# Reordering the first batch of a fused attention and feed-forward kernel: loads, products and value copies

## The chip, the cores and the metric

The kernel runs on one core of a Trainium2 chip. The metric is the device time of one execution in microseconds. Five engines work side by side, each through its own instruction queue in order: TensorE (PE, matmuls and transposes into PSUM), VectorE (DVE), ScalarE (ACT), GpSimd (POOL) and SyncE (SP). GpSimd and SyncE also issue the transfers (DMAs) between device memory and the on-chip memory SBUF; the loads that turn float32 into bfloat16 are all issued by GpSimd.

## What is computed

Eight batches of windowed attention, eight heads of 64 channels, 576 tokens each, followed by a feed-forward layer over all 4608 tokens. Heads 0 to 3 ("plain") see the 32 tokens up to their own; heads 4 to 7 ("dilated") see every fourth token back, 32 of them.

```python
scores = scale * np.matmul(q, k.transpose(0, 1, 3, 2))
mask_plain = (rel >= 0) & (rel < window)                       # window 32
mask_dil = (rel >= 0) & (rel < window * dilation) & (rel % dilation == 0)   # dilation 4
...
attn = np.exp(scores); attn = attn / (np.sum(attn, axis=-1, keepdims=True) + 1e-09)
x = attn_out.transpose(0, 2, 1, 3).reshape(B * S, H * D)       # 4608 x 512
h = np.maximum(x @ w_in, 0.0)                                  # w_in 512 x 2048
return (h * h @ w_out).astype(np.float32)                      # w_out 2048 x 512
```

## The kernel before

The four head pairs are numbered e = 0 to 3; pairs 0 and 1 are plain, 2 and 3 dilated. The attention output of pair e is rows kt = e of a transposed activation `xT`, so a feed-forward matmul (line 939) multiplies one pair's rows (kt) with 128 columns of `w_in`; four of them, kt 0 to 3, complete a piece. Its results pass a relu on ScalarE (line 952) and a square on VectorE (line 955), and the second layer (line 986) multiplies them with `w_out`.

The first batch is cut into part 0 (tokens 0 to 255) and part 1 (the other 320). The feed-forward layer starts with tiles of 256 tokens. The function `ffn_groups` gives a tile's work as a list of groups. In the first tile a unit u is two pieces of 128 columns, and the first six groups are halves: group 0 does units 0 and 1 with kt 0 and 1 (the plain pairs), group 1 the same units with kt 2 and 3, groups 2 and 3 units 2 and 3 likewise, groups 4 and 5 units 4 and 5. Group 16 is the first group of the second tile, tokens 256 to 511, with kt 2 and 3, and so needs part 1 of the dilated pairs. The lists at lines 1139 and 1140 set the order of the groups: 0, 1, 2, 3, 16, 4, 5, 17 and so on. Relu and square of units 0 and 1 of the first tile are held back, until the codes `r` (relus) and `R` (squares).

All else in the first batch is ordered by hand, in the text PROGRAM (line 21): codes, and a bar after which the next feed-forward group runs. Everything ahead of the first bar comes before group 0. Each engine takes its share of the codes in this order. The codes:

- `L0:q001` and the like (line 166): loads of q and of k of batch 0; the first digit is the part, the rest are pairs, so `q101` is part 1 of the plain pairs. Two DMAs each.
- `L0:v0d`, `L0:v1d` (line 197): values of the dilated pairs, part 0 and 1, two DMAs each into a staging tile `vd`; `L0:v1s`, `L0:v1t` (line 189): values of plain pair 0 and 1, part 1, straight into the block tile `vbd`, two DMAs each. `L0:i...` loads a quarter of w_in, with `a` or `b` half of its rows (line 1057), and `L0:o...` a quarter of w_out. `L0:i0` is the whole first quarter.
- `T`, `C`: transposes of q and k of one pair and part on TensorE, and the copies from PSUM; `C..a` puts the first copy on ScalarE, `C..v` on VectorE (lines 752 to 779). `B` and `S`: bias and scores; `E`: exponential on ScalarE, with a mask product on VectorE in part 1 (line 824); `P` and `D`: products with the values, and denominators; `L`, `X`, `M`: logarithm and exponential for the reciprocal on ScalarE, and the final product on VectorE into `xT` (line 884). A code's two digits are pair and part; L, X and M of pairs 0 and 2 in part 0 stand for both pairs of their kind.
- `G20` and the like: spreading of a dilated pair's staged values into `vbd` for part 1 (two copies of 64 x 256, line 229); the last digit is the part of the values, and part 1's products need both. `h`: casts of the plain values, part 0, into `vbd`. `N`, `z`, `y`: zeroing. `u` and `m`: masks of part 1 and others. `f`: a load of the mask for later batches, issued by SP. `w`, `W`, `s`: filler matmuls on zeros.

A tile in PSUM or SBUF comes from a pool with few buffers: the pool `pf` has four, which the scores of part 0, products, and the feed-forward units use in turn, and a new tile waits until the former user of its buffer is through. `pa` has two.

GpSimd's queue in the first 40 us holds the loads of batch 0, the weights, the first loads of batch 1, and the memsets `z` and `y`. SP's queue holds the plain values of part 0 (line 1025), two small value loads, the mask of `f`, and later stores and transposing DMAs (`L2:x` and so on).

Of the kernel before, what the change touches and what calls it, by code (L numbers as in the profile page):

```python
# [18 lines left out]


PROGRAM = (
    "L0:q001 L0:q023 L0:q123 L0:v0d L0:i0 L0:q101 L0:v1d L0:i1a L0:i1b L0:v1s L0:i2a L0:v1t L0:i2b L0:i3 L0:o0 L0:o1 L0:o2 L0:o3 "
    "L1:q00123 z y L1:v0dp L1:q10123 s34x151 T00 C00a T10 C10a B00 B10 w1 S00 E00 B20 W1 S10 E10 N u B30 W1 w1 T20q "
    "w1 T20k C20v T30 C30v h W1 w1 S20 E20 w1 S30 E30 T21 C21v T31 C31a G20 G30 P00 P10 D00 D10 L00 X00 P20 P30 "
    "D20 D30 L20 X20 M00 j S21 S31 w1+31 M20 E21 E31 G21 G31a | T01q T11q | T01k C01v r T11k C11a R P21 P31 D21 D31 S01 S11 L21 "
    "X21 M21 L31 X31 M31 E01 E11 | L2:q00123 L2:q10123 L1:v1dpr | | P01 D01 L01 X01 M01 P11 D11 L11 X11 M11 | | | "
    "| | | | | | | | | m n f | | | | | | 1q1 1q3 | 1q2f 1k2f | 1k1a 1v3 | 1a2 | 1v2 1k0a 1q0v | 1o2 | 1a0 1a1 | 1k3 "
    "1o0 1o1f | 1a3 1Q0 | 1K0 1o3 | 1Q1 1K1 | 1Q2 | 1b0 | | 1Q3 1K2 L2:vwp L3:q00123 L3:q10123 L2:vwdr | L2:x | | "
    "| | 1V2 | 1b2 1p0 | 1b1 1V3 1K3 | L3:x | 1p2 1p1f | 1b3 | 2t0 2t1 1p3f | | | L3:Vd0 L3:V1a L4:q00123 L4:q10123 "
    "L3:V1b | | | | | | | | | | L4:x | | | | | | | | | | | | | | | | | | L4:Vd L5:q10123 L5:q00123 L4:V01 | | | "  # L30
    "| | | | | | | | | | | | | L5:x | L5:Vd L6:q10123 L6:q00123 L5:V01"
# [31 lines left out]
def kernel(  # L63
# [9 lines left out]
    nc = tc.nc  # L73
# [28 lines left out]
    NF = DFF // P  # L102
# [57 lines left out]
    def staged(b: int, nm: str):  # L160


        t = rb[STAGE[b]][nm]
        return t[:, :].rearrange("p (a h x) -> p a h x", h=H, a=2)

    def load_qk(b: int, part, es):
        hs = slice(2 * es[0], 2 * es[-1] + 2)
        for nm, src in (("q", q), ("k", k)):
            t = staged(b, nm)
            t0, n = RES * MS[part], MN[part]  # L170
            nc.gpsimd.dma_start(  # L171
                t[0:n, part, hs, :], src[b, hs, t0 : t0 + RES * n, :].rearrange("h (p r) d -> p h (r d)", r=RES)
            )
# [50 lines left out]
    def spread_v(b: int, e: int, parts, copy=nc.vector.tensor_copy):  # L224

        p0, p1 = parts[0], parts[-1] + 1
        for hl in range(2):
            rows = slice(64 * hl, 64 * hl + 64)
            copy(
                vbd[b % 2][rows, e, RES * p0 : RES * p1, rows],  # L230
                vds[b][rows, e - NE // 2, p0:p1, :].rearrange("p m (r d) -> p (m r) d", d=D),
            )
# [200 lines left out]
    def step(b: int, code: str):  # L433

        what, e, home = code[0], int(code[1]), code[2:]
        part = int(what in "QKVbp")
        his = (0,) if "l" in home else (1,) if "h" in home else (0, 1)
        if what in "qk" and (b > XB or b == XB and e >= NE // 2):  # L440
            t = (qx if what == "q" else kx)[b % 2]
            halves(e, what, t[:, 2 * e : 2 * e + 2, :, :], 0, M, copier(what, e, home), his)
        elif what in "qQkK" and "h" in home:
            halves(e, what.lower(), *ready[b, e, what.lower()], his)
        elif what == "t":
            trans_both(e)
        elif what in "qQkK":
            trans(b, e, what.lower(), part, home)
        elif what in "vV":
            spread_v(b, e, [part] if b in PARTED else [0, 1])  # L450
        elif what in "ab":
            scores(b, e, part)
        elif "f" in home:
            pv(b, e, part, ps_f, "pf")
        else:
            pv(b, e, part)
# [265 lines left out]
    def turn(n: int, cols: int, at=None):  # L722


        if at:
            to = first["S", at[0], at[1]]
        else:
            to = first["W"] = first.get("W") or ps_o.tile([P, 512], f32, name="po")
        rhs = idle[:, :].unsqueeze(1).broadcast_to([P, cols // 256, 256]) if cols > 256 else idle[:, 0:cols]
        for _ in range(n):  # L730
            nc.tensor.matmul(
                to[:, 0:cols], idle[:, 0:P], rhs, start=not at, stop=not at, skip_group_check=True
            )
# [272 lines left out]
    def zero_halves(t):  # L1006
        nc.vector.memset(t[0:64, :, :, 64:128], 0.0)
        nc.vector.memset(t[64:128, :, :, 0:64], 0.0)
# [30 lines left out]
    def masks(part):  # L1039
        md = r4(mask_d[:, 256:704])  # L1040
        if part:
            put(r4(mask_p[:, 352:384]), near[:, :, 16:24])
            put(mask_p[:, 384:768].rearrange("p (i c) -> p i c", c=96), mk[:, 0:96].unsqueeze(1).broadcast_to([P, 4, 96]))
            put(r4(mask_p[:, 768:832]), near[:, :, 0:16])
            put(md[:, :, 0:32], mk[:, 224:256].unsqueeze(1).broadcast_to([P, RES, 32]))
            put(md[:, :, 32:112], mk[:, 160:240].unsqueeze(1).broadcast_to([P, RES, 80]))
            put(mask_d[:, 704:768], mk[:, 96:160])
            return
        put(mask_p[:, 0:288].rearrange("p (i c) -> p i c", c=96), mk[:, 0:96].unsqueeze(1).broadcast_to([P, 3, 96]))
        put(r4(mask_p[:, 288:352]), near[:, :, 0:16])  # L1050
        mf = mask_f[:, 0:320].rearrange("p (r c) -> p r c", r=2)
        put(mf[:, :, 0:80], mk[:, 176:256].unsqueeze(1).broadcast_to([P, 2, 80]))
        put(mf[:, :, 80:160], mk[:, 160:240].unsqueeze(1).broadcast_to([P, 2, 80]))
        put(mask_f[:, 320:384], mk[:, 96:160])
        put(r4(mask_d[:, 0:256]), mk[:, 160:224].unsqueeze(1).broadcast_to([P, RES, 64]))
# [20 lines left out]
    def run(code):  # L1076
        if code == "y":
            for nm in "qk":
                nc.gpsimd.memset(staged(1, nm)[64:80, 0, :, :], 0.0)
                nc.gpsimd.memset(staged(2, nm)[64:80, 0, 0 : H // 2, :], 0.0)  # L1080
        elif code == "z":
            nc.gpsimd.memset(vbd[1][0:64, :, :, 64:128], 0.0)
            nc.gpsimd.memset(vbd[1][64:128, :, :, 0:64], 0.0)
        elif code in "mu":
            masks(int(code == "u"))
        elif code == "R":
            while held:
                held.pop(0)[1]()
        elif code == "r":
            for relu, _ in held:  # L1090
                relu()
        elif code == "N":
            zero_halves(vbd[0][:, NE // 2 :, 0:8, :])
        elif code[0] == "G":
            spread_v(0, int(code[1]), [int(code[2])], nc.scalar.copy if code[3:] else nc.vector.tensor_copy)
        elif code == "h":
            for rows in sides:
                nc.vector.tensor_copy(vbd[0][rows, 0:2, 0:4, rows], plain[rows, :, :, :])
        elif code == "j":
            for rows in sides:  # L1100
                nc.vector.tensor_copy(vbd[0][rows, 2:4, 8, rows], tail[rows, :, :])
        elif code == "n":
            zero_halves(kbd)
        elif code == "f":
            nc.sync.dma_start(mask_n[:, :], near_dram.ap())
        elif code[0] == "s":
            turn(*(int(x) for x in code[1:].split("x")))
        elif code[0] in "wW":
            n, _, at = code[1:].partition("+")
            turn(int(n), 512 if code[0] == "w" else 256, [int(x) for x in at])  # L1110
        elif code[0] in "TCBSEPDXM" or code[0] == "L" and code[2:3] != ":":
            first_step(code)
        elif code[0] != "L":
            step(int(code[0]), code[1:])
        else:
            b, what, part, which = int(code[1]), code[3], code[4:5], code[5:]
            if what == "V":
                load_v_rows(b, code[4:] or "d01")
                return
            if what == "q":  # L1120
                load_qk(b, None if part == "w" else int(part), [int(e) for e in which])
            elif what == "x":
                cross_all(b)
            elif what == "v":
                load_v(b, [0, 1] if part == "w" else [int(part)], which)
            else:
                (load_w_in if what == "i" else load_w_out)(int(part), *[which][: len(which)])
# [6 lines left out]
    groups, steps = [], []  # L1134
# [1 line left out]
        groups += ffn_groups(tk0, nt)  # L1136

    head = groups[:G]
    groups[:NF] = [head[y] for y in (0, 1, 2, 3, 16, 4, 5, 17, 18, 19, 20, 21, 6, 7, 22, 23)]
    groups[NF:G] = [head[y] for y in (8, 9, 12, 13, 10, 11, 14, 15)] + head[24:32]  # L1140
    for x, code in enumerate(("R00", "R01", "R10", "R11")):
        steps.append((46, 0, XB, code))
# [5 lines left out]
    for b in range(NATURAL, B):  # L1148
# [12 lines left out]
        if b < PAIRED:  # L1161
            start = 61 if early else t - 8
            second = t + (7 if early else 5)
            x = 3 if early else 0
# [89 lines left out]
```

## Time and profile before

| | us |
|---|---|
| median of 3 runs | 299.52 (299.28 to 300.28) |
| the profiled execution | 298.59 |
| its span in the profile | 296.8 |
| TensorE busy | 289.8 (98%) |
| VectorE / ScalarE / GpSimd busy | 166.8 / 192.0 / 129.2 |
| first feed-forward matmul | 14.55 after the span's start |
| start of the fifth feed-forward group (units 4 and 5) | 23.09 |

All times inside an execution are counted from the start of its span. A timeline line gives start, length, engine, line of the kernel, operation, what is written from what, and in brackets the engine's idle time before it with what released it. The chain of waits goes back from the last instruction, at each step to what released it. A load's landing is the time at which its last byte was there.

### The profile page before, as it was taken

How to read it: one execution, taken by the hardware profiler on the slowest of the kernel's cores; microseconds unless marked ns; L12 is line 12 of the kernel's file. 1: busy time of each engine (PE TensorE's matmuls, PEld its weight loads, DVE VectorE, ACT ScalarE, POOL GpSimd, SP SyncE). 2: the span in 40 equal slices, each digit the busy share in tenths (PEclk: the TensorE clock that was granted, in tenths of full speed). 3: DMA queues.
4: the chain of work that ended last, by engine and by line, in shares of the span. 5: the costliest groups of instructions: out<-in, count | busy, mean ns of one | idle time of the engine just before them, and what ended most of it. 6: DMA issues, size and time to landing. Idle time of an engine off the chain costs nothing.

```text
span 296.8 us, 7869 instructions
## 1 busy us (share of the span) xinstructions
PE 289.8 (98%) x3156; PEld 169.7 (57%) x3183; DVE 166.8 (56%) x508; ACT 192.0 (65%) x397; POOL 129.2 (44%) x210
## 2 busy tenths in 40 slices
PE   8999999999999999999999999999999999999995
PEld 7689657868755554555455445545554455445543
DVE  2785566967869565686749474957445234005400
ACT  6897568757958665888667667766676567126511
POOL 8689882686695265855883687100000000000000
PEclk9999999999999999999999999999999999999999
DMA  8999999999989999979999599112101200121022
GB/s 126 202 188 213 204 152 229 182 163 186 180 101 172 195 130 178 155 128 173 167 195 148 66 171 170 11 38 73 38 0 33 77 35 0 38 71 35 0 74 71
DMA packets 82964, 35.37 MB, mean 119 GB/s; under 512 B 52608, under 2 KB 78176, under 8 KB 82928
## 3 DMA queue, kind: packets, MB, share of 16 engines
q0 software_dynamic: 49024, 18.40, 54.9%
q1 hardware_dynamic: 33760, 16.38, 27.8%
q8 instruction: 25, 0.41, 0.6%
q10 hardware_dynamic: 144, 0.10, 0.1%
q14 instruction: 11, 0.09, 0.1%
HBM read 37.31 MB, written 9.44 MB: 157 GB/s over the span
## 4 chain that ended last, share of the span: by engine, by line
PE 91%; DMA 4%; issue 1%; ACT 1%; POOL 1%; DVE 0%; ACTq 0%; POOLq 0%
PE pf L939 42%; PE pf L986 41%; DMA vd<-in_v_dram 2%; DMA kb<-in_k_dram 2%; PE po L661 2%; PE pf L661 1%; PE pa L661 1%; PE pd L661 1%; PE pa L277 1%; ACT h2T L952 0%; POOL qb L171 0%; PE po L414 0%; PE pa L357 0%; PE pa L351 0%; PE pd L416 0%
## 5 line engine op out<-in xcount | busy, mean ns | idle before, releaser
L986 PE MATMUL pf<-w_out_sb,h2T 128*128 128x512 bf16 (+2 forms) x572 | 127.5, 373 | 1.3 <-issue 0.5
L939 PE MATMUL pf<-xT,w_in 128*128 128x512 bf16 (+1 forms) x697 | 128.0, 340 | 0.6 <-DVE xT L884 0.2
L939 PEld LDWEIGHTS <-w_in 128*128 128x128 bf16 x704 | 77.9, 113 | 46.6 <-issue 0.5
L952 ACT ACTIVATE h2T<-pf 128x512 bf16<-128x512 f32 x144 | 83.7, 600 | 29.2 <-PE pf L939 28.8
L955 DVE TENSOR_TENSOR h2T<-h2T 128x512 bf16<-128x512 bf16 x144 | 60.2, 424 | 60.0 <-ACT h2T L952 57.6
L986 PEld LDWEIGHTS <-h2T 128*128 128x128 bf16 x592 | 55.5, 98 | 61.6
L992 ACT COPY osb<-pf 128x512 f32<-128x512 f32 (+1 forms) x34 | 19.5, 574 | 49.7 <-PE pf L986 49.6
L478 POOL DMA_DIRECT2D vbd<-in_v_dram x80 | 42.9, 546 | 20.0 <-DMA qb<-in_q_dram 7.1
L171 POOL DMA_DIRECT2D qb<-in_q_dram x18 | 13.0, 722 | 12.7 <-DMA xx<-qb 11.0
L684 ACT ACTIVATE rec<-rec 128x576 f32<-128x576 f32 x24 | 16.4, 682 | 0.7
L698 ACT ACTIVATE pt<-pa 128x384 bf16<-128x384 f32 (+1 forms) x28 | 12.7, 498 | 6.1 <-DVE xT L689 3.6
L192 POOL DMA_DIRECT2D vbd<-in_v_dram x16 | 11.0, 693 | 8.1 <-DMA kb<-in_k_dram 3.8
L687 DVE TENSOR_TENSOR xT<-po,rec 128x512 bf16<-128x512 f32 x14 | 9.7, 691 | 7.6 <-ACT rec L684 7.3
L465 POOL DMA_DIRECT2D vd<-in_v_dram x20 | 12.1, 614 | 3.8 <-PE pf L661 1.1
L171 POOL DMA_DIRECT2D kb<-in_k_dram x18 | 12.8, 710 | 1.5 <-issue 1.0
L470 POOL DMA_DIRECT2D vbd<-in_v_dram x20 | 11.9, 611 | 3.2 <-PE pf L939 1.1
L700 DVE TENSOR_TENSOR pt<-pt,mask_n 128x448 bf16<-128x448 bf16 (+1 forms) x20 | 7.1, 373 | 9.5 <-ACT pt L698 9.4
L700 DVE TENSOR_TENSOR pt<-pt,mask_f 128x384 bf16<-128x384 bf16 x24 | 8.4, 355 | 6.0 <-ACT pt L698 5.9
L687 DVE TENSOR_TENSOR xT<-pf,rec 128x512 bf16<-128x512 f32 x10 | 6.9, 692 | 8.7 <-ACT rec L684 8.7
L492 DVE COPY qT<-xx 64x576 bf16<-64x576 bf16 (+1 forms) x30 | 10.5, 349 | 0.6
L661 PEld LDWEIGHTS <-vbd 64*64 64x64 bf16 x288 | 7.6, 107 | 4.2 <-issue 3.8
L698 ACT ACTIVATE pt<-pf 128x448 bf16<-128x448 f32 (+1 forms) x18 | 8.5, 521 | 0.5 <-PE pf L661 0.3
(156 smaller groups left out, 317.0 us busy)
## 6 DMA issues: line engine op xcount, KB each, us to landing
qb<-in_q_dram POOLq DMA_DIRECT2D x7, 320.0 KB, 6.7
kb<-in_k_dram POOLq DMA_DIRECT2D x7, 320.0 KB, 8.1
vd<-in_v_dram POOLq DMA_DIRECT2D x32, 64.0 KB, 6.1
w_out_sb<-in_moe_w_out_dram POOLq DMA_DIRECT2D x4, 512.0 KB, 10.6
out_dram<-osb SPq DMA_DIRECT2D x16, 128.0 KB, 4.6
qb<-in_q_dram POOLq DMA_DIRECT2D x7, 256.0 KB, 8.5
kb<-in_k_dram POOLq DMA_DIRECT2D x7, 256.0 KB, 9.1
out_dram<-osb SPq DMA_DIRECT2D x9, 160.0 KB, 3.9
```

The lines of the kernel that those rows point to most:

```text
L171: nc.gpsimd.dma_start(t[0:n, part, hs, :], src[b, hs, t0 : t0 + RES * n, :].rearrange("h (p r) d -> p h (r d)", r=RES))
L478: nc.gpsimd.dma_start(v_rows[b % 2][p0 + 16 * r : p0 + 16 * r + 16, e, :, :], v[b, 2 * e + hl, :, :].rearrange("(i m r) d -> r m i d", r=R ...
L661: nc.tensor.matmul(out, lhs, rhs, start=begin, stop=True, skip_group_check=True)
L684: nc.scalar.activation(rec[:, :], rec[:, :], ACT.Exp, scale=-1.0)
L687: nc.vector.tensor_tensor(out=tok[:, :, 16:M], in0=byr(o[:, :]), in1=byr(rec[:, 0:512]), op=ALU.mult)
L698: nc.scalar.activation(pt, sp[b, e][g][:, 0:n], ACT.Exp, scale=SCALE)
L700: nc.vector.tensor_tensor(out=pt, in0=pt, in1=mask, op=ALU.mult)
L939: nc.tensor.matmul(to, w_in_sb[piece][:, kt, c0 : c0 + 509 : 4], rhs, start=(kt == kts[0] and x == 0), stop=(kt == kts[-1] and x == per - ...
L952: nc.scalar.activation(hv, acc[u][:, :].rearrange("p (x n) -> p x n", x=per), ACT.Relu)
L955: nc.vector.tensor_tensor(out=hv, in0=hv, in1=hv, op=ALU.mult)
L986: nc.tensor.matmul(cur[m][:, c0:c1], h2[:, f, P * m : P * m + P], w_out_sb[:, f, c0:c1], start=(f == 0), stop=(f == NF - 1),)
L992: (nc.vector.tensor_copy if last and part == 1 or tk0 == 3 * NT // 2 else nc.scalar.copy)(osb[:, c0:c1], cur[m][:, c0:c1])
```

## The change

- The first quarter of w_in is loaded in two halves (`i0a`, `i0b`), the staged dilated values of part 1 (`v1d`) come ahead of plain q and k of part 1 (`q101`).
- Three of the four spreads of dilated values move to GpSimd: `G20p` and `G30p` between the loads `i1b` and `v1s`, `G21p` between `v1s` and `i2a`. They were on VectorE (six copies). The fourth, `G31a`, stays on ScalarE.
- `h` comes ahead of B30; the plain products of part 0 (`P00 P10 D00 D10 L00`) come ahead of the dilated scores S20, S30 and of the transposes of part 1 of the dilated pairs (`T21`, `T31`); three fillers go; C31 is on VectorE.
- After group 1 come the relus, the dilated products of part 1, the squares, and only then the transposes of plain q and k of part 1, which stood before and after group 1. The plain scores of part 1 (`S01`, `S11`) stand after group 2, no longer before it.
- Group 16 comes ahead of group 3.
- `f` goes from among the first feed-forward groups to behind `L2:x`. SP ran it at 4.85 us, since nothing held it there.

```diff
-    "L0:q001 L0:q023 L0:q123 L0:v0d L0:i0 L0:q101 L0:v1d L0:i1a L0:i1b L0:v1s L0:i2a L0:v1t L0:i2b L0:i3 L0:o0 L0:o1 L0:o2 L0:o3 "
-    "L1:q00123 z y L1:v0dp L1:q10123 s34x151 T00 C00a T10 C10a B00 B10 w1 S00 E00 B20 W1 S10 E10 N u B30 W1 w1 T20q "
-    "w1 T20k C20v T30 C30v h W1 w1 S20 E20 w1 S30 E30 T21 C21v T31 C31a G20 G30 P00 P10 D00 D10 L00 X00 P20 P30 "
-    "D20 D30 L20 X20 M00 j S21 S31 w1+31 M20 E21 E31 G21 G31a | T01q T11q | T01k C01v r T11k C11a R P21 P31 D21 D31 S01 S11 L21 "
-    "X21 M21 L31 X31 M31 E01 E11 | L2:q00123 L2:q10123 L1:v1dpr | | P01 D01 L01 X01 M01 P11 D11 L11 X11 M11 | | | "
-    "| | | | | | | | | m n f | ...
+    "L0:q001 L0:q023 L0:q123 L0:v0d L0:i0a L0:i0b L0:v1d L0:q101 L0:i1a L0:i1b G20p G30p L0:v1s G21p L0:i2a L0:v1t L0:i2b L0:i3 "
+    "L0:o0 L0:o1 L0:o2 L0:o3 L1:q00123 z y L1:v0dp L1:q10123 s34x151 T00 C00a T10 C10a B00 B10 w1 S00 E00 B20 W1 S10 E10 N u h "
+    "B30 W1 w1 T20q w1 T20k C20v T30 C30v P00 P10 D00 D10 L00 S20 E20 S30 E30 X00 T21 C21v T31 C31v P20 P30 D20 D30 L20 X20 M00 j "
+    "S21 S31 w1+31 M20 E21 E31 G31a | | r P21 P31 D21 D31 R T01q T11q T01k C01v L21 X21 T11k C11a M21 L31 X31 M31 | "
+    "S01 S11 E01 E11 L2:q00123 L2:q10123 L1:v1dpr | | P01 D01 L01 X01 M01 P11 D11 L11 X11 M11 | | | "
+    "| | | | | | | | | m n | ...
-    "... | L2:x | | "
+    "... | L2:x f | | "
...
-            spread_v(0, int(code[1]), [int(code[2])], nc.scalar.copy if code[3:] else nc.vector.tensor_copy)
+            spread_v(0, int(code[1]), [int(code[2])], {"a": nc.scalar.copy, "p": nc.gpsimd.tensor_copy}.get(code[3:], nc.vector.tensor_copy))
...
-    groups[:NF] = [head[y] for y in (0, 1, 2, 3, 16, 4, 5, 17, 18, 19, 20, 21, 6, 7, 22, 23)]
+    groups[:NF] = [head[y] for y in (0, 1, 2, 16, 3, 4, 5, 17, 18, 19, 20, 21, 6, 7, 22, 23)]
```

## The prediction

> **What bounds the kernel now.** First the page's busy table and clock row: is one engine full, and is its clock whole?
>
> ```profile
> PE 289.8 (98%) x3156; PEld 169.7 (57%) x3183; DVE 166.8 (56%) x508; ACT 192.0 (65%) x397; POOL 129.2 (44%) x210
> PEclk9999999999999999999999999999999999999999
> ```
>
> TensorE is busy 98% of the span at full clock, so whatever is gained or lost must be TensorE's idle or filler time. Asked in stretches, TensorE is busy 268.4 of the 273.7 us after 23.1 us. The order of the instructions after that point is not changed. I therefore ask one thing: when does the fifth feed-forward group of the first batch (its units 4 and 5) start? Before, that is 23.09 us, after which TensorE runs nearly solid. A later or earlier start is passed on to the end one to one.
>
> Second, the chain of waits up to 25 us (start, length, what):
>
> ```profile
> 3.20 5.79 DMA kb<-in_k_dram
> 9.27 7.06 DMA vd<-in_v_dram
> 16.36 0.41 ACT vbd L229
> 16.79 0.40 ACT vbd L229
> 17.21 0.25 ACT h2T L952
> 17.71 0.59 ACT h2T L952
> 18.30 0.33 ACT xx L775
> 18.65 0.50 DVE xx L776
> 19.19 0.42 PE pa L813 x11
> 19.61 2.75 PE pf L939 x24
> ```
>
> The chain is a transfer, not arithmetic: the second part of the dilated values (the load v1d) lands at 16.33, two ScalarE copies spread it, two held relus queue behind them, then a copy of plain k, then the plain scores at 19.19. Only from 19.6 does TensorE stay full.
>
> Third, TensorE's own timeline, to see what it does meanwhile:
>
> ```profile
> 14.55 1.03 PE L939 MATMUL pf<-xT,w_in 128*128 128x256 bf16 x8 [0.16 <-DVE xT L884]
> 15.52 0.48 PE L761 MATMUL pa<-mk,qb 80*64 80x80 bf16 x16
> 17.33 0.45 PE L851 MATMUL po<-pt,vbd 128*128 128x32 bf16 x9
> 19.19 0.42 PE L813 MATMUL pa<-xx 64*64 64x32 bf16 x12 [0.35 <-DVE xx L776]
> ```
>
> Transposes of plain q and k (15.52 and 16.92) fill the time until the spread values are there; the products of part 1 of the dilated heads start at 17.33.
>
> Fourth, GpSimd's timeline, since the change puts copies into its queue:
>
> ```profile
> 11.37 1.42 POOL L1060 DMA_DIRECT2D w_in<-in_moe_w_in_dram  x2 [0.78 <-DMA kb<-in_k_dram]
> 12.77 0.72 POOL L192 DMA_DIRECT2D vbd<-in_v_dram  x1
> 14.55 0.67 POOL L192 DMA_DIRECT2D vbd<-in_v_dram  x1 [1.05 <-DMA w_in<-in_moe_w_in_dram]
> 15.42 0.74 POOL L1060 DMA_DIRECT2D w_in<-in_moe_w_in_dram  x1 [0.20 <-issue]
> 16.28 1.36 POOL L192 DMA_DIRECT2D vbd<-in_v_dram  x2
> ```
>
> Each issue takes 0.6 to 0.8 us, and the ninth load on waits for the landing of the one eight earlier (the load at 14.55 waited for the whole first quarter of w_in, landed 14.2). So this queue runs at the pace of the DMA.
>
> **The change, part by part** (times on the profile's clock).
>
> *Loads.* With w_in's first quarter in two loads and v1d ahead of plain q and k (q101), the first eight issues stay; the two halves go at 6.27 and 7.05, v1d at about 8.0 and 9.27 (its waits for loads 3 and 4 remain), q101 at 9.9 and 11.37 (waits for load 6), w_in's second quarter at 12.05 and 12.75. The last ends at 13.45. One more load is issued (0.75 us), where the queue waited anyway. By landed bytes (about 190 KB per us between 11.6 and 19.5), the first half lands near 12.9, the second at 14.2 as before, v1d 320 KB sooner, at 14.6 and 15.0, and q101 near 16.6 instead of 16.0. Moving the near mask's load (112 KB, issued by SP at 4.85, landed 10.95) behind batch 2's transposes takes it out of the first loads' way: between 0 and 112 KB at 195 GB/s, or 0.6 us; I take 0.4. Its first reader is at 103.9, against some 60 for the new place: nothing lost. So GpSimd is free at 13.45 - 0.4 = 13.05.
>
> *Plain products first.* The plain value casts (h, 0.86) move to 8.47, when the memsets are through and their last load has landed (8.2), ending 9.33 just before the transposes that VectorE waits for anyway: no cost. P00 P10 D00 D10 (0.8) follow the transposes' end at 9.6 and take the place of two 512-column and one 256-column filler. The first Ln is at 10.45, behind it E20 and E30 (0.35 apart) to 11.75, X00 to 12.4. C31 goes from ScalarE (0.69) to VectorE: 12.12 to 12.8. So M00 is at 12.8 to 13.5, against 13.81 to 14.50: one microsecond sooner, and M20 ends at 14.65 instead of 15.65. The first feed-forward group runs from 13.75 (its half of w_in is there), the second from 14.7 to 15.7 (before: 15.93 to 16.95).
>
> *Copies on GpSimd.* This decides. The part 1 products need all three spreads, G21p last. In the queue: four copies, two v1s loads (0.72 + 0.67), two copies. The trace has no GpSimd copy. Rows near it:
>
> ```profile
> L1080 POOL MEMSET qb<- 16x1024 bf16 x1 | 0.9, 945 | 0.0
> L1079 POOL MEMSET qb<- 16x2048 bf16 x1 | 1.8, 1797 | 0.0
> ```
>
> The difference is 0.83 ns per element and the rest 0.09 us, so writing 256 elements costs 0.31 us; reading and writing in turn would be 0.52. ScalarE takes 0.40 for this very copy, VectorE 0.22 to 0.33. Ends 0.22 and 0.52; I take 0.40, the same shape on the other engine without a doubled rate, which lies midway between the memset bounds. VectorE works on two SBUF operands meanwhile (the mask products, two of 0.40): a mutual delay of 0 to 0.8, taken as 0.2, since only part of them falls on the copies. Sum: 13.05 + 1.6 + 1.39 + 0.8 + 0.2 + 0.05 hand-over = 17.1. TensorE, through with the second group at 15.7, waits 1.4 us, and part 1 starts 0.2 sooner than before instead of 1.6. The two VectorE spreads (1.01 and 0.65) are saved off the path. ScalarE's G31a now ends about 15.6 and the relus 16.7: no longer the limit.
>
> For the price of the copy, the Trainium skill, GPSIMD Engine Reference, sections 3.1 and 4.1, calls one-input work roughly line-rate and its best loop 1.8 cycles per element; at its 1.2 GHz an estimate of 0.38 us, by which the sum would end 0.1 us sooner. No run so far shows it.
>
> *From part 1 to the fifth group.* Before: 23.09 - 17.33 = 5.76 us. Added: both pairs of transposes, 0.82, which earlier filled the wait, now stand behind part 1. Gone: the 0.35 wait for plain k ahead of 19.19, since a group stands between. New: the group on part 1 (units 0 and 1 of the next 256 tokens) is moved ahead of one group and needs the PSUM buffer that M31 frees. ScalarE does L21, X21, C11, L31, X31 after part 1 (five of about 0.45, C11 waiting for its transposes), then M31 comes 3.97 after part 1 starts, and TensorE would be there at 3.5: 0.45 lost. Sum 5.76 + 0.82 - 0.35 + 0.45 = 6.68, rounded to 6.65.
>
> The fifth group then starts at 17.1 + 6.65 = 23.75, 0.66 later than before. Behind G21p, w_in's third quarter is issued at 17.05 instead of 15.42 and v1t at 17.8 and 18.5 instead of 16.28. With the landing time before (5.6 and 5.1), they land at 22.65 and 23.6, with the 3.4 of an early load at 21.9; v1t is wanted at 23.3. I count nothing, with 0.3 as the upper end. GpSimd's later memsets move by some 1 us, but at 36.15 it waits for w_out again.
>
> The profiled execution took 298.59 (span 296.8), the median run 299.52, 0.93 more. The sum gives 299.25 against the former; against the median **300.2**.
>
> **Rivals.** *One, slower: GpSimd as the bound.* Copies of 0.52, the full 0.8 of collisions and no gain from the mask: 13.45 + 3.12 + 1.39 + 0.8 + 0.05 = 18.8, so the fifth group at 25.45, +2.4, 301.9; v1t late adds 0.3 to 0.8. For it: six copies stand in front of loads wanted soon. Against: the memsets run at 0.83 ns per element. It decides (beyond 0.3%) from 17.35, that is from 0.44 us per copy. Beside it stands the Trainium skill, SBUF — State Buffer, section "Who interferes with whom": VectorE work with two SBUF inputs and GpSimd's reads exclude each other for a whole instruction. GpSimd only writes and issues before, so no row shows that.
>
> *Two, faster: the copies are short.* At 0.22 each and 0.6 from the mask: 12.85 + 1.32 + 1.39 + 0.05 = 15.6, so part 1 starts at 15.7 right behind group two, the fifth group at 22.35, -0.75, 298.8. Break-even is a start at 16.45, a copy of 0.29 at my other values. For it: VectorE's rows. Against: even a pure write has 0.31.
>
> *Three: the idle stretch costs clock.* The granted clock is 1.00 in every stretch of before, thanks to fillers in the waits; 1.4 us is now empty. If the next 3 us ran at half rate: +1.5 more, 301.7. Against: the stretch from 18 to 20 us holds only 1.65 us of work, and its clock is 1.00.
>
> **How the numbers follow.** A tell-apart of about 0.3% (0.9 us) is what such a measurement allows. The forecast (part 1 at 16.5 to 17.9) has 0.55: 0.33 within 0.9 us, 0.22 beyond, slower. Rival one 0.19, slower. Rival two 0.22: its full price is short of 0.9 us, but loads landing sooner than I count would pass it: 0.12 faster, 0.10 same. Rival three 0.04, slower. Faster 0.12, same 0.43, slower 0.45. The range runs from rival two to rival one, 298.8 to 301.9; the forecast's own is 299.6 to 301.0.
>
> **What would show it.** First group near 13.75 and second ending near 15.7; six GpSimd copies near 0.4 us; an empty stretch on TensorE from 15.7 to about 17.1, released by GpSimd; M31 releasing the group after S11; the fifth group at 23.75. Copies under 0.3 or over 0.5 us, a wait of the fifth group or of P11 on a load, or a later stage that is not solid would make it wrong.

## The result and the profile after

| | before | after |
|---|---|---|
| median | 299.05 us (298.39 to 301.33, 22 runs) | 300.41 us (299.37 to 303.3, 22 runs) |
| ratio, with its 95% interval | | 1.0048 [1.0033, 1.0063] |
| start of the fifth feed-forward group (profiles) | 23.09 | 23.50, and 24.76 in a second profile |
| second half of w_in's third quarter issued, landed | 17.63, 22.9 | 19.23, 26.5 |

The change costs 1.36 us. The first profile of the changed kernel is of the slowest of its 22 runs (303.30 us, span 301.5); a second one, of a run at 300.11 us, stands below under "again". First the same two lines of the page as before, busy times and granted clock by fortieths of the span:

```profile
PE 292.6 (97%) x3180; PEld 170.1 (56%) x3180; DVE 166.5 (55%) x503; ACT 191.9 (64%) x396; POOL 132.7 (44%) x217
PEclk9997999999999999999999999999999999999999
```

The clock row has one digit below 9, in the fourth slice (22.6 to 30 us). Before it had none. GpSimd is busy 3.5 us longer. The chain of waits up to 27 us (start, length, what):

```profile
11.69 1.41 POOL w_in L1060 x2
...
13.15 0.40 POOL vbd L229
...
14.89 1.32 POOL vbd L192 x2
...
16.71 0.48 POOL vbd L229
17.20 0.68 POOL w_in L1060
17.88 1.35 POOL vbd L192 x2
19.23 7.29 DMA w_in<-in_moe_w_in_dram
26.51 0.05 issue
26.56 0.62 PE pf L939 x2
```

Read it upwards from the last line. TensorE's sixth group waited for a load of w_in; that load was issued at 19.23 because GpSimd's queue had been working through copies and other issues without a pause since 11.7. Before, the chain went through the staged values and ScalarE, and no load of w_in stood in it. These two lines of before are the ones to compare with, GpSimd's issue of the second half of that quarter (the first of the two) and TensorE's fifth group with all that follows it:

```profile
17.63 1.53 POOL L1060 DMA_DIRECT2D w_in<-in_moe_w_in_dram  x2
23.09 9.78 PE L939 MATMUL pf<-xT,w_in 128*128 128x256 bf16 x88
```

TensorE's timeline after the change shows the wait itself (start, length, operation, and in brackets the idle time before it and its releaser):

```profile
13.63 0.22 PE L813 MATMUL pf<-xx,kbd 64*64 64x64 bf16 x2 [0.90 <-issue]
14.31 1.91 PE L939 MATMUL pf<-xT,w_in 128*128 128x256 bf16 x16
17.25 0.42 PE L851 MATMUL po<-pt,vbd 128*128 128x80 bf16 x8 [1.02 <-POOL vbd L229]
23.50 1.04 PE L939 MATMUL pf<-xT,w_in 128*128 128x256 bf16 x8
26.56 10.58 PE L939 MATMUL pf<-xT,w_in 128*128 128x256 bf16 x80 [2.01 <-DMA w_in<-in_moe_w_in_dram]
```

Part 1 of the dilated heads starts at 17.25 behind GpSimd's last copy, and the fifth group at 23.50, only 0.41 later than before. Then, where there had been 9.78 us of solid work in 88 matmuls, eight run, TensorE stands for 2.01 us, and the other 80 take 10.58 us instead of 8.92 (the length they have in runs below at full clock). GpSimd's timeline:

```profile
13.15 1.74 POOL L229 COPY vbd<-vd 64x256 bf16<-64x256 bf16 x4
14.84 1.38 POOL L192 DMA_DIRECT2D vbd<-in_v_dram  x2
16.26 0.94 POOL L229 COPY vbd<-vd 64x256 bf16<-64x256 bf16 x2
17.14 0.74 POOL L1060 DMA_DIRECT2D w_in<-in_moe_w_in_dram  x1
17.88 1.38 POOL L192 DMA_DIRECT2D vbd<-in_v_dram  x2
19.23 1.53 POOL L1060 DMA_DIRECT2D w_in<-in_moe_w_in_dram  x2
```

The copies take 0.40 us each with 0.04 between them. w_in's third quarter goes out in two halves, at 17.14 and 19.23; before it was 15.42 and 17.63. The second half also took longer from issue to landing, 7.3 us instead of 5.3, and between 18 and 24 us the DMA carried 117 GB/s, where before it carried 185. Why the landing took longer is open. It is not the late issue alone: in the table below, three kernels that issue this half at 17.57 to 17.93 wait 6.2 to 6.9 us for it, and one that issues it at 18.62 waits 5.4.

### The profile page after: what moved, and what is told of

It is laid out like the page before. It is cut to its first block, busy times and chain, and to the rows that moved or that the text cites. A ratio compares the mean times of both kernels' runs of the same rounds, so it can differ in the third digit from the quotient of the medians.

```text
span 301.5 us, 7891 instructions
## 1 busy us (share of the span) xinstructions
PE 292.6 (97%) x3180; PEld 170.1 (56%) x3180; DVE 166.5 (55%) x503; ACT 191.9 (64%) x396; POOL 132.7 (44%) x217
## 4 chain that ended last, share of the span: by engine, by line
PE 83%; DMA 10%; POOL 5%; issue 1%; ACT 0%; POOLq 0%; ACTq 0%
PE pf L986 39%; PE pf L939 37%; DMA kb<-in_k_dram 6%; DMA w_in<-in_moe_w_in_dram 2%; DMA vbd<-in_v_dram 2%; PE po L661 2%; POOL vbd L192 1%; PE pf L661 1%; PE pa L661 1%; POOL qb L171 1%; POOL vbd L229 1%; PE pd L661 1%; POOL w_in L1060 1%; PE pa L277 1%; POOL kb L171 0%
## 5 line engine op out<-in xcount | busy, mean ns | idle before, releaser
L939 PE MATMUL pf<-xT,w_in 128*128 128x512 bf16 (+1 forms) x704 | 130.4, 344 | 2.2 <-DMA w_in<-in_moe_w_in_dram 2.0
L986 PE MATMUL pf<-w_out_sb,h2T 128*128 128x512 bf16 (+2 forms) x592 | 129.3, 373 | 0.0
L478 POOL DMA_DIRECT2D vbd<-in_v_dram x80 | 43.3, 551 | 18.8 <-DMA qb<-in_q_dram 7.6
L698 ACT ACTIVATE pt<-pa 128x384 bf16<-128x384 f32 (+1 forms) x28 | 12.8, 500 | 6.1 <-DVE xT L689 3.6
## 6 DMA issues: line engine op xcount, KB each, us to landing
w_out_sb<-in_moe_w_out_dram POOLq DMA_DIRECT2D x4, 512.0 KB, 12.4
```

The costliest lines, as they stand in the source:

```text
L478: nc.gpsimd.dma_start(v_rows[b % 2][p0 + 16 * r : p0 + 16 * r + 16, e, :, :], v[b, 2 * e + hl, :, :].rearrange("(i m r) d -> r m i d", r=R ...
L698: nc.scalar.activation(pt, sp[b, e][g][:, 0:n], ACT.Exp, scale=SCALE)
L939: nc.tensor.matmul(to, w_in_sb[piece][:, kt, c0 : c0 + 509 : 4], rhs, start=(kt == kts[0] and x == 0), stop=(kt == kts[-1] and x == per - ...
L986: nc.tensor.matmul(cur[m][:, c0:c1], h2[:, f, P * m : P * m + P], w_out_sb[:, f, c0:c1], start=(f == 0), stop=(f == NF - 1),)
```

## Experiments

Theory: the cost is the place of the copies in GpSimd's queue. They push back the issue of w_in's third quarter, whose second half had about one microsecond in hand (landed 22.9; the sixth group, 1.04 us after the start of the fifth, would have wanted it at 24.1). Rivals: the work of the copies costs by itself, each its share; the later start of part 1; the new order on the other engines; the idle stretches and the clock. In the diffs a line of code letters is cut to the part that differs. All ratios are against runs of the kernel before on the same chip.

| kernel | second half of third quarter issued, landed | fifth group | TensorE's waits after that, us | profiled run minus start of fifth group | ratio |
|---|---|---|---|---|---|
| before | 17.63, 22.9 | 23.09 | none | 275.50 | 1 |
| two spreads on GpSimd | 17.34, 22.6 | 22.82 | none | 275.72 | 1.0007 |
| fewer fillers | 17.57, 24.5 | 24.59 | none | 275.60 | 1.0017 |
| new order, copies on VectorE | 17.71, 24.5 | 23.78 | 1.14 for w_out | 277.70 | 0.9995 |
| mask late | 17.81, not recorded | 23.27 | none | 275.56 | 0.9974 |
| load order alone | 17.93, 24.1 | 23.52 | none | 275.58 | 0.9997 |
| mask twice | 18.51, 24.4 | 24.00 | 0.55 for w_out | 276.54 | 1.0027 |
| order alone | 18.62, 24.0 | 25.04 | none | 275.43 | 1.0043 |
| transposes in the gap | 18.78, 25.1 | 23.74 | 0.30 for w_in | 276.25 | 1.0046 |
| again | 19.12, 25.3 | 24.76 | none | 275.35 | 1.0042 |
| after | 19.23, 26.5 | 23.50 | 2.01 for w_in | 279.80 | 1.0048 |
| copies alone | 19.30, 25.7 | 23.06 | 1.64 for w_in, 0.30 for w_out | 277.95 | 1.0058 |
| hold the queue | 19.36, 26.7 | 23.82 | 1.89 for w_in | 277.64 | 1.0067 |
| last spread on GpSimd | 19.75, 26.0 | 24.07 | 0.95 for w_in | 276.83 | 1.0054 |

Below the kernel before, the table is sorted by the issue of that half. No kernel that issues it by 17.93 has an interval above 1; all that issue it from 18.5 on have. (In "order alone" and "mask twice" TensorE did not wait for it; there an earlier landing was late, which held up TensorE and this queue alike.) The last but one column confirms the way of reading of the prediction: where TensorE waits for nothing later, the time is the start of the fifth group plus 275.35 to 275.72 us.

**The changed kernel again.** No edit.

> The changed kernel once more, for a second profile. Start theory (part 1 of the dilated heads starts at 17.2 with TensorE idle from 16.1, the transposes stand behind it; the fifth feed-forward group is 0.4 us late and nothing more): the stall of the sixth group on w_in, 2.0 us in the first profile, is a stray of that execution and is under 0.5 us here; about 300.0. Queue theory (the GpSimd copies push the issue of w_in's third quarter from 15.42 and 17.63 to 17.14 and 19.23, so its second half lands after the sixth group wants it, near 24.4): the stall is here again, 0.5 to 2 us; about 300.4, ratio 1.0045.

Measured: 300.11 us (299.79 to 300.74), ratio 1.0042 [1.0027, 1.0058]. TensorE's timeline of this run:

```profile
14.45 0.22 PE L813 MATMUL pf<-xx,kbd 64*64 64x64 bf16 x2 [1.86 <-issue]
15.13 3.40 PE L939 MATMUL pf<-xT,w_in 128*128 128x256 bf16 x16
24.76 9.78 PE L939 MATMUL pf<-xT,w_in 128*128 128x256 bf16 x88
```

The wait for w_in is gone, but only because the fifth group is late for other reasons: TensorE stands 1.86 us for nothing that the profile names, the clock then falls and the first sixteen feed-forward matmuls take 3.40 us instead of 1.91. The half landed at 25.3, the sixth group began at 25.8. So one execution loses the time at 13 us, another at 24.5, and both end late. Neither theory expected this: the start theory has the missing wait right, but not the time, and the queue theory the time, but not the missing wait. Whatever TensorE does, the sixth group can't start before 25.3 to 26.5.

**The copies on VectorE again.** The changed kernel with the three spreads off GpSimd:

```diff
-L0:i1b G20p G30p L0:v1s G21p L0:i2a
+L0:i1b L0:v1s L0:i2a
-M20 E21 E31 G31a |
+M20 G20 G30 E21 E31 G21 G31a |
```

> The changed kernel with the three spreads back on VectorE, behind M20 (G20, G30) and behind the masks of part 1 (G21); all else as changed. Part 1 still starts near 17.1, so the start theory and the order theory expect the time of the change, ratio 1.003 to 1.005. Queue theory: GpSimd's queue issues w_in's third quarter at its old times, the stall is gone: 0.5 to 2 us less than the change, ratio 0.999 to 1.001.

Measured: 298.73 us (298.07 to 301.48), ratio 0.9995 [0.9968, 1.0023]. Undoing the copies alone takes the whole cost away. TensorE and GpSimd:

```profile
16.60 0.72 PE L851 MATMUL po<-pt,vbd 128*128 128x32 bf16 x9
23.78 9.78 PE L939 MATMUL pf<-xT,w_in 128*128 128x256 bf16 x88
```

```profile
17.71 0.77 POOL L1060 DMA_DIRECT2D w_in<-in_moe_w_in_dram  x1
```

Part 1 starts 0.65 earlier than with the copies on GpSimd, and the third quarter is out in time. The profiled run is the slowest of this kernel, with a wait of 1.14 for w_out at 39 us.

**The copies on GpSimd alone.** The kernel before, its order kept, with the three spreads in the queue:

```diff
-L0:i1a L0:i1b L0:v1s L0:i2a
+L0:i1a L0:i1b G20p G30p L0:v1s G21p L0:i2a
-C31a G20 G30 P00
+C31a P00
-E31 G21 G31a |
+E31 G31a |
```

> The kernel before, with G20, G30 and G21 on GpSimd at the places that the change gives them, and nothing else of it. Queue theory: the second half of w_in's third quarter is issued at about 19.4 instead of 17.63 and lands near 25, wanted at 23.97: TensorE stalls 0.5 to 2 us on w_in, 299.6 to 301, ratio 1.002 to 1.007. Start theory: G21 ends about 17.2 and part 1 starts at 17.33 as before, no stall: ratio 0.999 to 1.001. Order theory (the new order itself costs, whoever copies): ratio 1.000.

Measured: 300.49 us (298.9 to 304.49), ratio 1.0058 [1.0038, 1.0078]. GpSimd, then TensorE:

```profile
16.35 0.93 POOL L229 COPY vbd<-vd 64x256 bf16<-64x256 bf16 x2 [0.79 <-DMA vd<-in_v_dram]
...
19.30 1.55 POOL L1060 DMA_DIRECT2D w_in<-in_moe_w_in_dram  x2
```

```profile
17.55 0.45 PE L851 MATMUL po<-pt,vbd 128*128 128x32 bf16 x9
...
25.73 8.92 PE L939 MATMUL pf<-xT,w_in 128*128 128x256 bf16 x80 [1.64 <-DMA w_in<-in_moe_w_in_dram]
```

The copies alone make the whole cost, with part 1 only 0.22 later than before (17.33) and the fifth group on time at 23.06. A late part 1 is therefore not the cause.

**Holding the queue without the copies.** The kernel before, copies on VectorE; GpSimd instead fills a scratch tile that nothing reads (`H`), four times ahead of v1s and three times behind it, 0.42 us each:

```diff
+        elif code == "H":
+            nc.gpsimd.memset(mask_f[:, :], 0.0)
-L0:i1a L0:i1b L0:v1s L0:i2a
+L0:i1a L0:i1b H H H H L0:v1s H H H L0:i2a
```

> The kernel before, all copies where they were; GpSimd's queue is held by memsets of a scratch tile instead (0.41 us each by the memset rows): four behind i1b, three behind v1s. Nothing reads them. Queue theory (time in GpSimd's queue ahead of w_in's third quarter is the whole cost): its halves are issued near 17.1 and 19.2 as with the copies, the second lands near 25.5, the sixth group stalls 1 to 2 us, ratio 1.004 to 1.007, as pool_copies_alone. Port theory (the copies themselves, by sharing SBUF with VectorE or by their data coming late, are the cost): ratio 0.999 to 1.001.

Measured: 301.28 us (300.5 to 302.89), ratio 1.0067 [1.0045, 1.009]. GpSimd, then TensorE:

```profile
12.75 1.87 POOL L1082 MEMSET mask_f<- 128x384 bf16 x4
...
19.36 1.53 POOL L1060 DMA_DIRECT2D w_in<-in_moe_w_in_dram  x2
```

```profile
26.76 8.93 PE L939 MATMUL pf<-xT,w_in 128*128 128x256 bf16 x80 [1.89 <-DMA w_in<-in_moe_w_in_dram]
```

Work that no one waits for costs as much as the copies, within the intervals. What counts is that the queue is occupied in front of the third quarter's load. The fifth group was at 23.82 in this profile, 0.73 later than before, so not all of the profiled time is the wait for w_in.

**Four copies against two.** If the work of the copies counted, four would cost more than two. If the queue counts, it is the other way about, since the four lie where the queue had to wait for a landing anyway, and the two must themselves wait for the staged values. Both are the kernel before with one part of the move:

```diff
-L0:i1b L0:v1s L0:i2a
+L0:i1b G20p G30p L0:v1s L0:i2a
-C31a G20 G30 P00
+C31a P00
```

```diff
-L0:i1b L0:v1s L0:i2a
+L0:i1b L0:v1s G21p L0:i2a
-E31 G21 G31a |
+E31 G31a |
```

> The kernel before with only G20 and G30 on GpSimd, behind the second quarter's second half; G21 stays on VectorE. Queue theory (the cost is how late w_in's third quarter is issued): the four copies take 1.74 us, but the next load but one had to wait until 14.55 us anyway, so the third quarter's first half goes at about 16.0 us, its second half at about 18.2 and lands at about 23.5, while it is wanted at about 23.9: no stall in TensorE's sixth group, ratio 0.999 to 1.002. Rival (each copy on GpSimd costs its share of what six cost, 0.58%): four copies give 1.004.

> The kernel before with only G21 on GpSimd, behind the load of plain values v1s; G20 and G30 stay on VectorE. Queue theory: the two copies are only 0.9 us of work but must wait for the landing of the dilated values at about 16.3 us, and everything behind them in the queue waits too; the third quarter's first half is issued at about 17.2 us, the second at about 19.3, as with all six copies, and TensorE waits 1 to 2 us for it: ratio 1.004 to 1.007. Rival (each copy costs its share): two copies give 1.002.

Measured: the four copies (G20, G30) 299.07 us, ratio 1.0007 [0.9994, 1.002]; the two (G21) 300.5 us, ratio 1.0054 [1.0038, 1.0069]. Of the kernel with four copies, GpSimd's lines:

```profile
11.69 1.74 POOL L229 COPY vbd<-vd 64x256 bf16<-64x256 bf16 x4
...
15.26 0.73 POOL L1060 DMA_DIRECT2D w_in<-in_moe_w_in_dram  x1 [0.32 <-DMA qb<-in_q_dram]
```

and of the kernel with two, GpSimd's and then TensorE's:

```profile
16.87 0.85 POOL L229 COPY vbd<-vd 64x256 bf16<-64x256 bf16 x2 [1.17 <-DMA vd<-in_v_dram]
17.66 0.74 POOL L1060 DMA_DIRECT2D w_in<-in_moe_w_in_dram  x1
```

```profile
26.06 8.92 PE L939 MATMUL pf<-xT,w_in 128*128 128x256 bf16 x80 [0.95 <-DMA w_in<-in_moe_w_in_dram]
```

1.74 us of copies cost nothing measurable: the queue reached the third quarter at 15.26, not later than before (15.42), though 16.0 had been expected. 0.85 us of copies, with 1.17 us of waiting in front of them in an ordered queue, cost 0.54%. The interval of the first excludes the share that its rival gave it (1.004), that of the second excludes 1.002. So it is the place in the queue that costs, not the work of the copies.

**The plain transposes back into the gap.** The changed kernel, with the transposes of plain q and k of part 1 ahead of the dilated products again, so that TensorE has work while it waits for GpSimd:

```diff
-G31a | | r P21 P31 D21 D31 R T01q T11q T01k C01v L21 X21 T11k C11a M21
+G31a | T01q T11q | r T01k C01v T11k C11a P21 P31 D21 D31 R L21 X21 M21
```

> The changed kernel with the transposes and copies of plain q and k of part 1 ahead of part 1's dilated products again (q behind group 0, k behind group 1), where TensorE waits for the spreads. Order theory: the 0.8 us of transposes go into the wait, the fifth group starts 0.6 to 0.8 us sooner, ratio about 1.002. Queue theory: the fifth and sixth group come sooner and wait longer for the same load, so the time stays, ratio 1.004 to 1.006.

Measured: 300.06 us (299.83 to 301.0), ratio 1.0046 [1.0029, 1.0063], as the changed kernel. TensorE's timeline:

```profile
21.07 1.80 PE L939 MATMUL pf<-xT,w_in 128*128 128x256 bf16 x15 [0.47 <-DVE xT L884]
...
25.08 8.93 PE L939 MATMUL pf<-xT,w_in 128*128 128x256 bf16 x80 [0.30 <-DMA w_in<-in_moe_w_in_dram]
```

The time is what the queue theory expected. But in the profiled execution the fifth group did not come sooner (23.74 against 23.50): TensorE stood 1.09 us at 12.8 for nothing that the profile names, then waited 0.33 for plain q and 0.47 for M31. So this run agrees with w_in's landing (25.1 here) as the limit of the sixth group, but does not show it.

**The load order alone.** The kernel before with the halves of w_in's first quarter and v1d ahead of q101:

```diff
-L0:i0 L0:q101 L0:v1d L0:i1a
+L0:i0a L0:i0b L0:v1d L0:q101 L0:i1a
```

> The kernel before with the new order of loads alone: w_in's first quarter in two halves, v1d ahead of q101; all else as before. Chain theory (the landing of v1d at 16.33 set the start): v1d lands about 1.5 sooner, ScalarE's spread and the held relus 1.2 to 1.5 sooner, the plain scores 0.4 sooner, the fifth group 0.3 to 0.6 sooner: ratio 0.998 to 0.999. Supply theory (from 18 us on the loads of w_in set the pace, with about 1 us of reserve at the second half of the third quarter): the same 0.998 to 0.999, never below 0.996. If q101, later by 0.6, is the limit: ratio 1.000 to 1.002.

Measured: 299.09 us (298.12 to 299.71), ratio 0.9997 [0.9984, 1.001]. The interval decides neither for the two theories (0.998 to 0.999) nor for plain q as the limit (1.000 to 1.002). What the dilated values gain, plain q loses:

```profile
16.49 0.48 PE L761 MATMUL pa<-mk,qb 80*64 80x80 bf16 x16 [0.67 <-DMA qb<-in_q_dram]
```

**The near mask late, and twice.** Two opposite edits of the kernel before: its 112 KB load behind batch 2's transposes; and the early load issued a second time, into a tile that is not used until later.

```diff
-m n f |
+m n |
-| L2:x |
+| L2:x f |
```

```diff
             nc.sync.dma_start(mask_n[:, :], near_dram.ap())
+            nc.sync.dma_start(xx[1][:, 0, 0:448], near_dram.ap())
```

> The kernel before with only the load of the later batches' mask moved behind batch 2's transposing DMAs. Expected by the reckoning of the prediction: the first loads land up to 0.4 sooner (load 6 at 10.6 instead of 11.04), TensorE's first wait is shorter, but the later chain hangs on v1d: 0 to 0.3 us gained, ratio 0.999 to 1.000. Rival: the transfer in mid-kernel runs into the transposing DMAs: ratio up to 1.002.

> The kernel before with the near mask's early load by SP issued a second time, into a tile that is not used until later (work that nothing reads, 112 KB). If the mask's early load costs time because it runs beside the first loads (as leaving it out of that place gave 0.9974), doubling it costs about as much again: ratio 1.002 to 1.003. If the gain came from something else (a changed instruction stream, a later place in SP's queue), 1.000 within 0.001.

Measured: late 298.44 us (298.06 to 299.08), ratio 0.9974 [0.9961, 0.9986]; twice 299.62 us (298.81 to 302.65), ratio 1.0027 [1.0006, 1.0049]. Taking the load out of the first transfers gains 0.26%, or 0.8 us; doubling it costs as much. The first is more than the 0.999 to 1.000 expected, the second is in the range expected, and the two together show that the load's presence there is the cause. TensorE's timeline with the mask twice shows where:

```profile
15.22 1.06 PE L939 MATMUL pf<-xT,w_in 128*128 128x256 bf16 x8 [0.35 <-DMA w_in<-in_moe_w_in_dram]
...
24.00 9.78 PE L939 MATMUL pf<-xT,w_in 128*128 128x256 bf16 x88
```

In this profile the first quarter of w_in lands late, all that follows shifts, and the fifth group starts 0.91 later than before. The single profile with the mask late (fifth group 23.27, in a run of 298.83 us) doesn't show the gain; it shows only in the medians. This edit alone makes a kernel that is faster than both.

**The new order alone.** The changed kernel with the three other parts undone: copies on VectorE (as above), loads in the old order, mask early.

```diff
-L0:v0d L0:i0a L0:i0b L0:v1d L0:q101 L0:i1a
+L0:v0d L0:i0 L0:q101 L0:v1d L0:i1a
-| m n |
+| m n f |
-| L2:x f |
+| L2:x |
```

> The new order of TensorE's, ScalarE's and VectorE's work alone: the kernel after, with the three spreads back on VectorE, the loads in the order of before and the near mask early again. If the parts add up (after +0.48%, of which copies +0.58, mask -0.26, loads -0.03, hence order +0.19): ratio 1.001 to 1.003. With the copies on VectorE and all else new it was 0.9995, so with the mask early 1.002. If the order is neutral and the mask's gain does not carry over into it: 1.000.

Measured: 300.18 us (299.84 to 300.5), ratio 1.0043 [1.0027, 1.0059]. The median is above what either reckoning gave, but the interval reaches down into the range of the first (1.001 to 1.003). So the parts may not add up; the noise leaves it open. TensorE:

```profile
13.26 0.44 PE L851 MATMUL po<-pt,vd 64*64 64x64 bf16 x15 [1.31 <-DMA vd<-in_v_dram]
...
15.35 3.59 PE L939 MATMUL pf<-xT,w_in 128*128 128x256 bf16 x16 [0.28 <-DMA w_in<-in_moe_w_in_dram]
```

The new order asks for the staged values of part 0 at 11.7, earlier than before (12.4). With the old loads their second half landed at about 13.2 in this run, TensorE stood, the clock fell, and two groups took 3.59 us. The fall of the clock is not a matter of this one execution: all five runs have a mean granted clock of 0.993 or 0.994, as the profiled executions with a stretch at half clock have (0.994), while 11 of the 12 runs of the same order with the new loads and the late mask are at 0.997 or more. Such a stretch costs 1.7 us of work (last section), and the whole loss is 1.28 us. With the new loads and the late mask the same order gave 0.9995. So in this order the two are worth some 0.5% together, where alone in the old order they gave 0.03% and 0.26%. Which of the two it needs wasn't tried apart, and that the wait for the staged values brings the clock down rests on one profile.

**Fewer fillers.** The kernel "copies on VectorE" with 24 fewer filler matmuls at the start of TensorE's work, to see whether its stand for nothing that the profile names belongs to a place or to a count:

```diff
-s34x151
+s10x512
```

> copies_on_vector with the 34 fillers of 151 columns turned into 10 of 512 (the same columns within 0.3%, 48 instructions fewer on TensorE). In the four profiles with the new order TensorE stands 0.9 to 1.9 us at one and the same instruction in the scores of part 1 of pair 2, for nothing that the profile names. Instruction theory (its instruction stream is not there yet; a transfer of kind instruction lies at 11 to 13 us): the gap goes from there and turns up 48 instructions later, in the first feed-forward groups, at most 0.9 long; ratio 0.995 to 0.999. Wait theory (it waits for a copy of k): the gap stays at the same scores, ratio as copies_on_vector, 0.9995.

Measured: 299.46 us (298.06 to 302.23), ratio 1.0017 [0.9994, 1.0041]. The stand left the scores and came 24 matmuls later in the work:

```profile
15.45 2.96 PE L939 MATMUL pf<-xT,w_in 128*128 128x256 bf16 x13 [1.90 <-issue]
```

The instruction theory has the place right: the stand follows the count of TensorE's instructions, not the work. It has the rest wrong: 1.90 us where at most 0.9 was expected, and a time no better than that of the kernel it was made from (1.0017, where 0.995 to 0.999 was expected). The wait theory is refuted, since the stand left the scores.

## Why the prediction was right or wrong

The time was forecast as 300.2 us and is 300.41; but the forecast difference was 0.66 us and the measured one is 1.36. The two misses nearly cancel: the difference was 0.70 too small, and the three runs shown of before had a median 0.47 above that of the 22. So the closeness of the number is luck. The cost that the forecast priced, a later fifth group, is 0.41 us of the first profile (in the second it is 1.67, but behind a stand of TensorE and a fall of its clock); the experiments put the cost at a place that the forecast counted as nothing. By the bound of 0.3% the change is slower, which had 0.45; the point forecast lay in "the same", which had 0.43.

- *The fifth group's start is passed on one to one*: right, within 0.4 us in seven profiles; but it is not the only thing that counts.
- *GpSimd free at 13.05, six copies of 0.40 us, part 1 at 17.1*: right. The copies start at 13.15 and take 0.40 each, part 1 starts at 17.25 after 1.02 us of empty TensorE, released by GpSimd. (The first group was at 14.31, not 13.75, since TensorE stood 0.90 us for nothing that the profile names; so the empty stretch is shorter than the 1.4 forecast.) The Trainium skill, GPSIMD Engine Reference, sections 3.1 and 4.1, from which an estimate of 0.38 was worked out, agrees with the trace. Of the Trainium skill's page SBUF — State Buffer, section "Who interferes with whom", little is seen: the last copy took 0.48 instead of 0.40, and two mask products on VectorE beside copies 1.05 us where before they took 0.79, about what the forecast set aside (0.2).
- *6.65 us from part 1 to the fifth group*: 6.25. The 0.45 that M31 was to cost did not come (it did, 0.47, where the transposes went back into the gap). The fifth group was at 23.50 against 23.75.
- ***"Behind G21p ... I count nothing, with 0.3 as the upper end"***: this term failed. For v1t itself it held: TensorE waited for it only in the kernel with two copies, 0.35 us. The forecast had the issues right (third quarter 17.05 forecast, 17.14 measured; v1t 17.8 and 18.5, measured 17.88 and about 18.5). But it followed the queue only as far as v1t, and left out the next entry, the second half of the third quarter. That was issued at 19.23 instead of 17.63 and was wanted at 24.5, 5.3 us later: exactly its landing time before, with nothing in hand. It took 7.3 here and 6.2 in the second profile. The term was worth up to 2.01 us of waiting, and putting the copies back on VectorE moves the ratio from 1.0048 to 0.9995.
- *The mask: 0.4 us, between 0 and 0.6*: probably too small. Alone, in the kernel before, it is worth 0.26%, or 0.8 us, with an interval from 0.4 to 1.2. The change without it was not run.
- *Rival one (GpSimd as the bound by copies of 0.52)*: its mechanism is refuted by the copies' length; but its sentence "six copies stand in front of loads wanted soon" names the place where the time went.
- *Rival two (short copies)*: refuted, 0.40 against 0.22.
- *Rival three (an idle stretch costs clock, 0.04)*: it happens in both profiles of the changed kernel, though behind other stretches than the one I named: behind the wait for w_in in one, behind the stand at 12.6 us in the other. So the argument against it, from a stretch of before with 1.65 us of work in 2, was too weak. But it is not what the change costs: of its 22 runs, five have a mean granted clock of 0.992 to 0.994, with a median of 300.45 us, and the other 17 are at 0.998 or more, with a median of 300.37. Nor did the 301.7 that this rival gave come.

## What to carry to other kernels

When work is put into a queue that also issues loads, list every load behind it down to the one with the least time in hand, and compare its new issue plus a landing time with some reserve (the same load took 5.3 to 7.4 us in these profiles) with the moment it is wanted; the first load behind it may have time, the third may not. The price of an instruction in such a queue is not its length: 1.74 us of copies where the queue waited anyway cost nothing measurable, 0.85 us behind a wait for data cost 0.5%. And a small load that nobody wants yet can matter among the first transfers: moving it was worth 0.26%, while the whole change with its copies back on VectorE, that move included, gained nothing measurable (0.9995).

## What the runs showed of the hardware

**The clock falls in blocks of 3.4 us.** Four of the fourteen profiles have a stretch at a granted clock of 0.50, all with the new order, and each is 3.4 us long: 26.6 to 30.0 (after), 15.4 to 18.8 (again and order alone), 15.1 to 18.5 (fewer fillers). Busy times of the changed kernel by stretches (stretch, length, then busy time and number of instructions of PE, PEld, DVE, ACT and POOL; then granted clock, DMA share, GB/s):

```profile
23.20:26.60 3.40, 1.39 (x22) 1.12 (x19) 1.63 (x4) 1.85 (x5) 3.36 (x3) 1.00 1.08 170
26.60:30.00 3.40, 3.40 (x17) 2.41 (x18) 0.85 (x2) 1.42 (x3) 3.35 (x3) 0.50 1.11 217
```

In the 3.4 us ahead, TensorE had been busy 1.39, 1.54, 1.85 and 1.85 us. So each block follows 3.4 us that were about half busy, and costs 1.7 us of work at full clock. The mean granted clock of these four executions is 0.994, that of the ten others 0.998 or more (3.4 of 298 us at half clock make 0.994), so a mean of 0.994 in a run without a profile is a sign of such a block. A block does not always follow: with the queue held, TensorE stood 1.89 us and was busy 1.51 of the 3.4 us from 24.0, and the clock stayed at 1.00; likewise with 1.64 us in the kernel with the copies alone. The Trainium skill, TensorE: Matmul & The Clock Gate, Part 1, describes a free-running activity window of about 3.4 us after which the clock is halved when the window was idle. The length agrees with the traces; here windows need not have been idle, and that the two exceptions had their pause divided between two windows would fit, but no run shows where the windows lie.

**TensorE can stand for nothing that the profile names.** For 0.90, 1.86, 1.17, 1.09 and 1.90 us in the five profiles of the new order without a wait for data just ahead, 0.23 and 0.53 in two of the old, TensorE stands at the same count of instructions, though not at the same work: by the timelines, in all seven profiles, just behind the 223rd matmul of the execution. With 24 fewer fillers that is 24 matmuls later in the work. One transfer of the kind "instruction" (0.02 MB) lies between 10 and 14 us in every profile, that of before too, which shows no such stand. An instruction supply that runs dry where TensorE gets ahead would fit that; this is argued, not shown.
